# Gate rows made by TensorE transposes and stored as whole rows, and the weights' check as one tensor_reduce

## The chip, the cores and the metric

The kernel runs on one core of a Trainium2 chip. The time is device microseconds of one launch, from host buffers already in the device's memory to the finished output. The kernel before takes 1070.4 us, the median of 3 runs (1067.88 to 1073.14).

## The reference

Three layers follow each other. The first is attention over 4 batches, 8 heads, 768 positions and 64 channels, with a window of 96 local keys, 8 global keys and a distance bias. The second is a dense layer on 3072 tokens, where `cos` stands for the activation. The third is a mixture of 8 experts with a skip gate. The gate rows of the change are the 8 columns of `w_gate` and the vector `w_skip`, nine vectors of 512 numbers in all.

```python
scores = scale * np.matmul(q, k.transpose(0, 1, 3, 2))      # masked, biased, softmax over keys
x = attention(q, k, v)                                      # 3072 x 512
h = x @ w_in;  g = h * np.cos(h);  x = g @ w_out            # d_ff = 2048
skip_score = x @ w_skip
logits = x[skip_score > 0] @ w_gate                         # 8 experts, argmax picks one
out = x;  out[do] += gate_w * (relu(x @ w1[e]) @ w2[e])
```

The weights `w_in` and `w_out` reach the kernel as 64-bit floats and are turned into 32-bit floats on the chip. The check of the change belongs to that: it notes, for every piece of weights, how small its smallest absolute value is, so that a slower path can be taken for values too small for the fast conversion.

## The kernel before

Tokens are worked on in 8 units (u = 0 to 7) of 384 tokens. Attention takes a unit's heads in 4 pairs (p = 0 to 3). For a pair, `att_Tq` and `att_Tk` turn Q and K over on TensorE, `att_S` multiplies them (6 products, each reduced by VectorE on L380), `att_E` takes exponentials on ScalarE and scales on GpSimd (L404), `att_P` turns the result over, and `att_V` multiplies it with V. I write S(2) for the products of unit 0's pair 2, and likewise V(3), and so on; pair p of unit 1 is (1,p).

Unit 0's attention runs first, as a prologue. Then `unit(0)` does 16 steps f of the dense layer: 12 matmuls into `hp` (L499), the activation, 9 matmuls into `zp` (L538). In the steps of one unit the next unit's attention is interleaved. While unit 0 runs, the weights are converted, in 32 pieces of 128x512 numbers. A piece is loaded into a tile `st` (L202, 4 buffers). `convert` then runs ScalarE on L210, and VectorE on L216 (the check), L223 and L227; `convert_end` adds on GpSimd (L234). Step f waits for its pieces, so unit 0 is the unit in which conversion and the dense layer go side by side. From unit 1 on the weights lie in SBUF.

The gate rows are loaded as columns into `wgs` (L736 and L737) and written to a DRAM tile `wg_t` (L739), whence one broadcast load brings them as rows to all partitions after unit 0 (`wrep`, L833).

All loads of the prologue stand in one queue, issued by SyncE in order; one issue waits for the DMA that stands eight before it, and for its buffer. A scheduler sets the order on SyncE, VectorE and GpSimd, also in the prologue on ScalarE and TensorE; TensorE's order from unit 0 on, and ScalarE's in the units, is as written.

Of the kernel before, what the change touches and what calls it, by code (L numbers as in the profile page):

```python
# [9 lines left out]
F32 = mybir.dt.float32  # L10
F32R = mybir.dt.float32r
BF16 = mybir.dt.bfloat16
# [3 lines left out]
ALU = mybir.AluOpType  # L16
AX = mybir.AxisListType
# [3 lines left out]
P = 128  # L21
# [16 lines left out]
def kernel(  # L38
    ctx, tc, q, k, v, n_global, n_local, w_in, w_out, w_skip, w_gate, w1, w2, out
):  # L40
    nc = tc.nc
    B, H, S, D = q.shape
    NT, DM = out.shape
    FF = w_in.shape[1]
    E, _, F2 = w1.shape
    NP = H // 2
    CC = DM // P
# [9 lines left out]
    NG = 16  # L57
# [5 lines left out]
    drp = ctx.enter_context(tc.tile_pool(name="drp", bufs=1, space=DRAM))  # L63
    ps_h = ctx.enter_context(tc.tile_pool(name="ps_h", bufs=2, space=PSUM))
    ps_z = ctx.enter_context(tc.tile_pool(name="ps_z", bufs=HT, space=PSUM))
    ps_a = ctx.enter_context(tc.tile_pool(name="ps_a", bufs=3, space=PSUM))
# [10 lines left out]
    ident = cpool.tile([P, P], F32, name="ident")  # L77
# [7 lines left out]
        out=upper, in_=ones, pattern=[[1, P]], base=0, channel_multiplier=-1,  # L85
        compare_op=ALU.is_gt, fill=0.0,
    )
    wgs = cpool.tile([P, CC, NG], F32, name="wgs")
# [12 lines left out]
    for j, a in enumerate((n_global, n_local)):  # L101
# [11 lines left out]
        out=lim, in0=lim_h, scalar=2.0 ** 32, in1=lim, op0=ALU.mult, op1=ALU.add  # L113
# [19 lines left out]
        out=loc, in0=rel, scalar=nlo, in1=dst, op0=ALU.is_lt, op1=ALU.mult  # L133
# [14 lines left out]
    def to_far(d, kept):  # L148
# [12 lines left out]
        out=dst_f, in0=tmp, scalar=nlo, in1=dst[:, 104:NW], op0=ALU.mult, op1=ALU.add  # L161
# [6 lines left out]
        out=dst[:, 0:8], in0=g8[:, 0:8], scalar1=nlo, scalar2=None, op0=ALU.mult  # L168
# [9 lines left out]

    xs = drp.tile([E * CAP, ROW], F32, name="xs")

    wg_t = drp.tile([E + 1, DM], F32, name="wg_t")

    def rows_of(e):
        return xs[e * CAP:e * CAP + NE, :].rearrange("(j p) r -> p j r", p=P)
# [13 lines left out]
    cmin = cpool.tile([P, 2 * FC], F32, name="cmin")  # L198
# [6 lines left out]
    def convert(st, dst, pool, n=None):  # L205
        def shaped(t):
            return t.rearrange("p (a b) -> p a b", b=P)

        b = pool.tile([P, 512], I32, name="cvb", bufs=2)
        nc.scalar.activation(out=b, in_=st[:, :, 0].bitcast(U32), func=AF.Copy, scale=2.0 ** -29)  # L210
        u = pool.tile([P, 512], BF16, name="cvu", bufs=2)
        hf = st[:, :, 1].bitcast(F32)
        if n is None:
            nc.scalar.activation(out=u, in_=hf, func=AF.Abs)
        else:
            nc.vector.tensor_tensor_reduce(  # L216
                out=u, in0=hf, in1=hf, op0=ALU.mult, op1=ALU.max, scale=-1.0, scalar=-3.0e38,
                accum_out=cmin[:, n:n + 1],
            )
        if dst is None:  # L220
            dst = shaped(st[:, :, 0]).bitcast(F32)
        hi, a = shaped(st[:, :, 1]), dst.bitcast(I32)
        nc.vector.tensor_scalar(  # L223
            out=a, in0=hi, scalar1=3, scalar2=0x3FFFFFF8,
            op0=ALU.logical_shift_left, op1=ALU.bitwise_and,
        )
        nc.vector.scalar_tensor_tensor(  # L227
            out=a, in0=hi, scalar=-0x40000000, in1=a, op0=ALU.bitwise_and, op1=ALU.bitwise_or
        )
        return dst, shaped(b), None if n is not None else shaped(u)  # L230
# [16 lines left out]
    def spare_tile():  # L247
        x = cp_.tile([P, 512, 2], I32, name="st", bufs=4).bitcast(F32)
        return x.rearrange("p n two -> p (n two)")
# [11 lines left out]
    def conv_tick():  # L261
        if len(conv_run) == 3 or (conv_run and conv_run[0][3] == 2):
            m, f, parts, _ = conv_run.pop(0)
            conv_done.add((m, f))
            if m == 1:
                hi, lo = (w[:, f].rearrange("p (a b) -> p a b", b=P) for w in (wo_hi, wo_lo))
                nc.scalar.copy(hi, parts[0])  # L267
                nc.vector.tensor_tensor(out=lo, in0=parts[0], in1=hi.bitcast(F32), op=ALU.subtract)  # L268
        for c in conv_run:
            if c[3] == 1:  # L270
                c[3] = 2
                convert_end(*c[2])
        conv_ahead(2)
        if conv_loaded:
            m, f, st = conv_loaded.pop(0)
            dst = work_place(f) if m else w_in_sb[:, :, f * P:(f + 1) * P]
            conv_run.append([m, f, convert(st, dst, cp_, 2 * f + m), 1])
        conv_ahead(1)
# [456 lines left out]
    att_load(0, 1)  # L735
    nc.sync.dma_start(wgs[:, :, 0:E], w_gate.rearrange("(c p) e -> p c e", p=P))  # L736
    nc.sync.dma_start(wgs[:, :, E:E + 1], w_skip.rearrange("(c p o) -> p c o", p=P, o=1))  # L737
    for e in range(E + 1):
        nc.sync.dma_start(wg_t[e].rearrange("(c p) -> p c", p=P), wgs[:, :, e])  # L739
    warm(16, ps_a, "ps")  # L740
    att_Tq(0, 0)
    att_Tk(0, 0)
    for p in range(NP + 1):
        if p + 1 < NP:
            att_Tq(0, p + 1)
            att_Tk(0, p + 1)
        if p < NP:
            for t in range(HT):
                att_S(0, p, t)
            if p + 1 < NP:  # L750
                fill(p + 1)
            if p + 2 < NP:
                att_load(0, p + 2)
            att_E(0, p)
        warm(2, ps_a, "ps")
        if p > 0:
            for t in range(HT):
                att_P(0, p - 1, t)
                if t > 0:
                    att_V(0, p - 1, t - 1)  # L760
            att_V(0, p - 1, HT - 1)
        conv_tick()

    def early():
        for s_ in range(min(list(ev) + list(late)), 0):
# [43 lines left out]
    is_low = cpool.tile([P, 2 * FC], BF16, name="is_low")  # L809
# [3 lines left out]
    def route_setup():  # L813
        nc.gpsimd.iota(slots, pattern=[[1, NE]], base=0, channel_multiplier=0,
                       allow_small_or_imprecise_dtypes=True)
        nc.gpsimd.iota(last_id, pattern=[[0, 1]], base=NT - P, channel_multiplier=1,
                       allow_small_or_imprecise_dtypes=True)
        side.close()
        rp_["p"] = route_pool.enter_context(tc.tile_pool(name="route", bufs=2, side="right"))

        nc.vector.tensor_scalar(
            out=is_low, in0=cmin, scalar1=-(1.125 * 2.0 ** -15) ** 2, scalar2=None, op0=ALU.is_gt
        )

        def count_low():
            lp = ps_a.tile([P, 2 * FC], F32, name="ps_w2", tag="ps")
            nc.tensor.matmul(lp, ones, is_low, start=True, stop=True)
            nc.vector.tensor_reduce(out=low, in_=lp, op=ALU.max, axis=AX.X)

        at(HS + 10, count_low)  # L830
        gp_ = rp_["g"] = gate_pool.enter_context(tc.tile_pool(name="gate", bufs=1, side="right"))
        wrep = gp_.tile([P, E + 1, DM], F32, name="wrep", bufs=1)
        nc.sync.dma_start(  # L833
            wrep.rearrange("p e d -> p (e d)"),
            wg_t.rearrange("(o e) d -> o (e d)", o=1).to_broadcast([P, (E + 1) * DM]),
        )
        Route.wrep = [wrep[:, e] for e in range(E + 1)]

# [91 lines left out]
    with tc.manual_schedule(engines={mybir.EngineType.PE}):  # L930
# [8 lines left out]
        with tc.manual_schedule(engines={mybir.EngineType.SP}):  # L939
            with tc.manual_schedule(engines={mybir.EngineType.Activation}):  # L940


                u = NU - 1
# [69 lines left out]
                with tc.manual_schedule(engines={mybir.EngineType.Pool, mybir.EngineType.DVE}):  # L1013
                    with tc.manual_schedule(engines={mybir.EngineType.Activation}):
# [17 lines left out]
                        def trans_x0(cs):  # L1032
# [16 lines left out]
                            out=sel, in0=slots, scalar1=r.sf[:, 0], scalar2=None, op0=ALU.is_equal  # L1049
# [15 lines left out]
                    for n in range(NS + LAG):  # L1065
                        e, f = divmod(n, F2C)
# [13 lines left out]
                        if n >= LAG:  # L1080
                            e, f = divmod(n - LAG, F2C)
# [35 lines left out]
        out=ctl[:, 1:2], in0=ctl[:, 4:5], scalar1=float(NE), scalar2=None, op0=ALU.is_gt  # L1117
# [276 lines left out]
```

## Time and profile before

| what | value |
|---|---|
| median of 3 runs | 1070.4 us |
| the profiled execution's own time | 1068.65 us |
| its span, first to last instruction | 1066.9 us |
| mean granted TensorE clock | 0.964 of full speed |
| busy TensorE / VectorE / GpSimd / ScalarE | 977.0 / 751.2 / 543.2 / 529.0 us |

The chain of work that ended last is 56% TensorE and 27% VectorE over the whole span, but that is an average over stages. The prologue lasts to 72.6 us, unit 0 to about 201.6 us. A busy figure counts an instruction from its start to its end, so one that stands still within counts as busy.

### The profile page before, as it was taken

How to read it: one execution, taken by the hardware profiler on the slowest of the kernel's cores; microseconds unless marked ns; L12 is line 12 of the kernel's file. 1: busy time of each engine (PE TensorE's matmuls, PEld its weight loads, DVE VectorE, ACT ScalarE, POOL GpSimd, SP SyncE). 2: the span in 40 equal slices, each digit the busy share in tenths (PEclk: the TensorE clock that was granted, in tenths of full speed). 3: DMA queues.
4: the chain of work that ended last, by engine and by line, in shares of the span. 5: the costliest groups of instructions: out<-in, count | busy, mean ns of one | idle time of the engine just before them, and what ended most of it. 6: DMA issues, size and time to landing. Idle time of an engine off the chain costs nothing.

```text
span 1066.9 us, 17010 instructions
## 1 busy us (share of the span) xinstructions
PE 977.0 (92%) x5673; PEld 806.2 (76%) x5673; DVE 751.2 (70%) x1867; ACT 529.0 (50%) x1278; POOL 543.2 (51%) x727
## 2 busy tenths in 40 slices
PE   6487787999998999999899999989998989999996
PEld 3265666777787788788677878877798879999995
DVE  5369899878569648855965795597456178888883
ACT  4366466655665666556556756656556111111110
POOL 2356877745444454544444445535546065556562
PEclk9578889999999999999999999999999999999998
DMA  6465445641121112112111211110003169555600
GB/s 65 98 193 151 126 131 144 182 149 27 39 70 25 36 47 68 27 40 66 29 29 48 63 30 39 39 45 14 11 30 145 53 232 353 191 195 194 214 23 23
DMA packets 135792, 98.28 MB, mean 92 GB/s; under 512 B 103959, under 2 KB 112151, under 8 KB 135568
## 3 DMA queue, kind: packets, MB, share of 16 engines
q1 hardware_dynamic: 132496, 91.13, 29.1%
q0 software_dynamic: 3200, 5.98, 1.5%
q8 instruction: 47, 0.77, 0.3%
q14 instruction: 49, 0.40, 0.1%
HBM read 80.58 MB, written 21.03 MB: 95 GB/s over the span
## 4 chain that ended last, share of the span: by engine, by line
PE 56%; DVE 27%; POOL 7%; issue 3%; DMA 2%; ACT 2%; SPq 1%; POOLq 0%; ACTq 0%; DVEq 0%
PE hp L499 14%; PE zp L538 14%; DVE junk L596 9%; PE hp L905 8%; PE zp L924 8%; DVE wi_lo L465 4%; POOL sc L404 3%; PE ps_s L375 3%; DVE cvu L216 2%; DVE r L482 2%; DVE sc L380 2%; DVE w_in_sb L223 2%; DVE r L525 2%; DVE w_in_sb L227 2%; POOL wi_hi L462 1%
## 5 line engine op out<-in xcount | busy, mean ns | idle before, releaser
L510 POOL TENSOR_TENSOR glo<-r,ghi 128x384 fp32r<-128x384 f32 x115 | 128.9, 1121 | 201.2 <-ACT ghi L509 200.9
L465 DVE TENSOR_TENSOR wi_lo<-w_in_sb,wi_hi 128x512 fp32r<-128x512 f32 x124 | 104.8, 845 | 117.1 <-POOL wi_hi L462 112.4
L499 PE MATMUL hp<-xhi,wi_hi 128*128 128x384 f32 x492 | 177.4, 361 | 9.0 <-DVE r L525 6.0
L499 PE MATMUL hp<-xhi,wi_lo 128*128 128x384 f32 x492 | 167.0, 339 | 2.7 <-DVE wi_lo L465 2.7
L499 PE MATMUL hp<-xlo,wi_hi 128*128 128x384 f32 x492 | 166.4, 338 | 0.0
L538 PE MATMUL zp<-wo_hi,ghi 128*128 128x512 f32 x345 | 148.9, 432 | 0.4 <-ACT wo_hi L267 0.4
L487 ACT ACTIVATE r<-r,halfpi 128x384 f32<-128x384 f32 x128 | 79.0, 617 | 134.8 <-DVE r L482 133.4
L596 DVE CUSTOM_DVE_ANT_0 junk<-r_zr,wrep 128x512 bf16<-128x512 f32 x162 | 139.1, 858 | 7.4 <-ACT r_zr L558 5.3
L538 PE MATMUL zp<-wo_hi,glo 128*128 128x512 f32 x345 | 138.7, 402 | 2.6 <-POOL glo L510 2.6
L538 PE MATMUL zp<-wo_lo,ghi 128*128 128x512 f32 x345 | 138.7, 402 | 1.4 <-DVE wo_lo L268 1.4
L404 POOL TENSOR_SCALAR sc<-sc,sm 128x232 f32<-128x232 f32 (+1 forms) x180 | 93.5, 538 | 75.5 <-DVE sm L399 60.1
L509 ACT CAST ghi<-r 128x384 fp32r<-128x384 f32 x115 | 58.9, 512 | 110.8 <-DVE r L525 110.1
L499 PEld LDWEIGHTS hp<-xhi,wi_hi 128*128 128x128 f32 x492 | 93.1, 189 | 25.6 <-issue 13.1
L462 POOL TENSOR_SCALAR wi_hi<-w_in_sb 128x512 fp32r<-128x512 f32 x128 | 92.0, 719 | 39.3 <-PE hp L499 34.0
L375 PE MATMUL ps_s<-kW,qT 64*128 64x232 f32 (+1 forms) x384 | 76.2, 416 | 25.0 <-DVE mx L380 11.2
L910 ACT ACTIVATE hh<-hp 128x256 fp32r<-128x256 f32 x64 | 24.5, 383 | 149.9 <-PE hp L905 149.9
L499 PEld LDWEIGHTS hp<-xhi,wi_lo 128*128 128x128 f32 x492 | 93.1, 189 | 3.4 <-DVE wi_lo L465 3.4
L499 PEld LDWEIGHTS hp<-xlo,wi_hi 128*128 128x128 f32 x492 | 93.4, 190 | 0.1
L394 ACT ACTIVATE sc<-sc,mx 128x232 f32<-128x232 f32 (+1 forms) x180 | 83.3, 464 | 4.3 <-DVE mx L380 3.9
L525 DVE TENSOR_TENSOR r<-r,hp 128x384 f32<-128x384 f32 x112 | 61.6, 550 | 33.5 <-ACT r L487 33.5
L843 POOL TENSOR_SCALAR w2h<-we 128x512 fp32r<-128x512 f32 x64 | 47.2, 738 | 69.4 <-PE zp L924 69.4
L538 PEld LDWEIGHTS zp<-wo_hi,ghi 128*128 128x128 f32 x345 | 66.7, 193 | 19.7 <-issue 8.6
(232 smaller groups left out, 2252.1 us busy)
## 6 DMA issues: line engine op xcount, KB each, us to landing
we<-in_moe_w_dram SPq DMA_DIRECT2D x16, 2048.0 KB
st<-in_moe_w_in_dram SPq DMA_DIRECT2D x16, 512.0 KB
st<-in_moe_w_out_dram SPq DMA_DIRECT2D x16, 512.0 KB
ld_q<-in_q_dram SPq DMA_DIRECT2D x64, 96.0 KB
ld_k<-in_k_dram SPq DMA_DIRECT2D x64, 96.0 KB
ld_v<-in_v_dram SPq DMA_DIRECT2D x64, 96.0 KB
out_dram<-r_zr SPq DMA_DIRECT2D x7, 768.0 KB
xs<-st SPq DMA_DIRECT2D x16, 257.0 KB
```

The costliest lines, as they stand in the source:

```text
L375: nc.tensor.matmul(sp[:, c0:NW], d["qT"][j * D:(j + 1) * D, t * P:(t + 1) * P], d["kW"][j * D:(j + 1) * D, t, c0:NW], start=True, stop=True,)
L394: nc.scalar.activation(out=s[:, j, c0:NW], in_=s[:, j, c0:NW], func=AF.Exp, scale=-1.0, bias=d["m"][:, t, j:j + 1], accum_out=sm[:, t, j:j ...
L404: nc.gpsimd.tensor_scalar(out=s[:, j, c0:NW], in0=s[:, j, c0:NW], scalar1=sm[:, t, j:j + 1], scalar2=1.0, op0=ALU.mult, op1=ALU.mult,)
L462: nc.gpsimd.tensor_scalar(out=hi, in0=ws, scalar1=1.0, scalar2=1.0, op0=ALU.mult, op1=ALU.mult)
L465: eng.tensor_tensor(out=lo, in0=ws, in1=hi.bitcast(F32), op=ALU.subtract)
L499: nc.tensor.matmul(hp, a[:, c, :], b[:, c, :], start=(n == 0), stop=(n == 3 * CC - 1))
L510: nc.gpsimd.tensor_tensor(out=glo, in0=r, in1=ghi.bitcast(F32), op=ALU.subtract)
L525: nc.vector.tensor_tensor(out=r, in0=r, in1=hp, op=ALU.mult)
L538: nc.tensor.matmul(zt[u][t], a[:, sl], b[:, f, :], start=(f == 0 and n == 0), stop=(f == FC - 1 and n == 2),)
L596: nc.vector.tensor_tensor_reduce(out=junk, in0=self.zr[:, t, 0:DM], in1=self.wrep[e], op0=ALU.mult, op1=ALU.add, scale=1.0, scalar=0.0, ac ...
L905: nc.tensor.matmul(hp, a[:, c, :], b[:, c, :], start=(n == 0), stop=(n == 3 * CC - 1))
L924: nc.tensor.matmul(yq[e][j], a[:, sl], b, start=(f == 0 and n == 0), stop=(f == F2C - 1 and n == 2),)
```

## The change

The check becomes a `tensor_reduce` with minimum over absolute values, which gives the least absolute value instead of the negated least square; the compare on L821 is adapted, and the scratch tile `cvu` is no longer allocated for it. The nine stores of gate columns (L739) go. In their place, after the prologue's loop, four transposes on TensorE turn the 16 columns of `wgs` into 16 rows of 512 in PSUM, ScalarE copies them into a borrowed `st` tile, and one DMA stores them to `wg_t`, which now has 16 rows.

```diff
         b = pool.tile([P, 512], I32, name="cvb", bufs=2)
         nc.scalar.activation(out=b, in_=st[:, :, 0].bitcast(U32), func=AF.Copy, scale=2.0 ** -29)
-        u = pool.tile([P, 512], BF16, name="cvu", bufs=2)
         hf = st[:, :, 1].bitcast(F32)
         if n is None:
+            u = pool.tile([P, 512], BF16, name="cvu", bufs=2)
             nc.scalar.activation(out=u, in_=hf, func=AF.Abs)
         else:
-            nc.vector.tensor_tensor_reduce(
-                out=u, in0=hf, in1=hf, op0=ALU.mult, op1=ALU.max, scale=-1.0, scalar=-3.0e38,
-                accum_out=cmin[:, n:n + 1],
+            nc.vector.tensor_reduce(
+                out=cmin[:, n:n + 1], in_=hf, op=ALU.min, axis=AX.X, apply_absolute_value=True
             )
...
-    for e in range(E + 1):
-        nc.sync.dma_start(wg_t[e].rearrange("(c p) -> p c", p=P), wgs[:, :, e])
     warm(16, ps_a, "ps")
...
+    gT = ps_a.tile([P, 512], F32, name="ps_g0", tag="ps")
+    for c in range(CC):
+        nc.tensor.transpose(gT[0:NG, c * P:(c + 1) * P], wgs[:, c, :], ident)
+    gr = spare_tile()[0:NG, 0:DM]
+    nc.scalar.copy(gr, gT[0:NG])
+    nc.sync.dma_start(wg_t, gr)
```

The scheduler orders the prologue anew around this. Below, lines of the changed kernel are mostly one lower than before (L302 is L301, L380 is L379). The first place is SyncE's queue behind the loads of `wgs`. Before, from the Q load of pair 2 on:

```order
L302 DMA ld_q<-in_q_dram 128x3x64 x2
L302 DMA ld_k<-in_k_dram 128x3x64
L739 DMA wg_t<-wgs 128x4x1 x9
L302 DMA ld_k<-in_k_dram 128x3x64
L310 DMA ld_va<-in_v_dram 8x2x64
L302 DMA ld_v<-in_v_dram 128x3x64 x2
```

The same place in the changed kernel:

```order
L301 DMA ld_q<-in_q_dram 128x3x64 x2
L301 DMA ld_k<-in_k_dram 128x3x64 x2
L202 DMA st<-in_moe_w_in_dram 128x4x256 x2
L301 DMA ld_q<-in_q_dram 128x3x64 x2
L301 DMA ld_k<-in_k_dram 128x3x64 x2
L202 DMA st<-in_moe_w_in_dram 128x4x256
```

The nine stores are gone from between the two halves of pair 2's K load, two pieces of weights follow at once, and Q and K of pair 3 come before V of pair 2.

The second place is GpSimd between the scaling of pair 1 (`xhi`) and that of pair 3 (`xlo`). Before:

```order
L404 TENSOR_SCALAR sc<-sc,sm 128x128 x2
L404 TENSOR_SCALAR sc<-sc,sm 128x232 x2
L234 TENSOR_TENSOR w_in_sb<-w_in_sb,cvb 128x4x128
L404 TENSOR_SCALAR sc<-sc,sm 128x232 x2
L462 TENSOR_SCALAR wi_hi<-w_in_sb 128x512
L234 TENSOR_TENSOR w_in_sb<-w_in_sb,cvb 128x4x128
L462 TENSOR_SCALAR wi_hi<-w_in_sb 128x512
L355 COPY kW<-keep 128x104
L356 COPY kW<-keep 128x2x8 x2
```

In the changed kernel:

```order
L233 TENSOR_TENSOR w_in_sb<-w_in_sb,cvb 128x4x128
L461 TENSOR_SCALAR wi_hi<-w_in_sb 128x512
L233 TENSOR_TENSOR w_in_sb<-w_in_sb,cvb 128x4x128
L461 TENSOR_SCALAR wi_hi<-w_in_sb 128x512
L355 COPY kW<-keep 128x2x8
L354 COPY kW<-keep 128x104
L355 COPY kW<-keep 128x2x8
L403 TENSOR_SCALAR sc<-sc,sm 128x128 x2
L403 TENSOR_SCALAR sc<-sc,sm 128x232 x4
```

The two conversion pieces and the small copies into `kW`, which S(3) needs, now stand ahead of the scaling of pair 2 (`sc`) and no longer behind it.

The third place is SyncE again, at the loads of unit 1's first pairs, in the changed kernel:

```order
L301 DMA ld_v<-in_v_dram 128x3x64 x2
L309 DMA ld_va<-in_v_dram 8x3x64
L766 DMA wg_t<-st 16x512
L314 DMA ld_va<-in_v_dram 96x3x64
L309 DMA ld_va<-in_v_dram 8x3x64
L314 DMA ld_va<-in_v_dram 96x3x64
L301 DMA ld_q<-in_q_dram 128x3x64 x2
```

The new store of the gate rows stands in the middle of pair (1,0)'s loads; pair (1,1), Q and K of pair (1,2) and the seventh piece of weights come behind it.

## Rows read from the trace of the kernel before

**Rows 1.** Waits, 14 to 72.6 us: who waited for whom; us, times, longest.
```profile
PE zp L341 <- DMA ld_k<-in_k_dram: 16.6, 1, 16.6
...
PE ps_s L375 <- POOL kW L356: 4.5, 1, 4.5
```

**Rows 2.** Chain that ended last, 14 to 75 us: start, us, what.
```profile
14.35 14.19 DMA wg_t<-wgs
28.55 9.11 DMA ld_k<-in_k_dram
...
37.79 0.89 PE zp L341 x3
...
54.42 2.78 PE ps_s L375 x8
...
67.98 0.47 DVE xlo L448
...
72.55 2.56 PE hp L499 x8
```

**Rows 3.** Stretches: range, length, busy per engine, granted clock, DMA share, GB/s.
```profile
14.00:38.00 24.00, 6.87 (x49) 4.21 (x49) 5.79 (x31) 6.28 (x25) 5.11 (x12) 0.70 0.53 22
38.00:72.60 34.60, 25.85 (x148) 17.11 (x147) 23.50 (x72) 19.83 (x63) 18.22 (x25) 0.70 0.59 158
72.60:201.60 129.00, 106.94 (x530) 82.20 (x530) 118.75 (x224) 77.93 (x179) 97.21 (x92) 0.87 0.49 142
201.60:1067.00 865.40, 827.21 (x4909) 697.85 (x4907) 595.58 (x1497) 419.64 (x1001) 420.24 (x583) 0.99 0.26 84
```

**Rows 4.** Timeline 0 to 30 us: start, us, engine, line, operation.
```profile
7.47 1.02 SPq L302 DMA_DIRECT2D ld_k<-in_k_dram  x2
...
10.78 0.55 PE L341 MATMUL zp<-ident,ld_k 128*128 128x128 f32 x3
```

**Rows 5.** Timeline of SyncE's issues, 10 to 240 us.
```profile
13.33 0.43 SPq L302 DMA_DIRECT2D ld_k<-in_k_dram  x1
13.86 10.37 SPq L739 DMA_DIRECT2D wg_t<-wgs  x9
...
65.50 1.00 SPq L302 DMA_DIRECT2D ld_q<-in_q_dram  x2
...
71.59 0.94 SPq L302 DMA_DIRECT2D ld_q<-in_q_dram  x2
...
73.71 0.42 SPq L202 DMA_DIRECT2D st<-in_moe_w_in_dram  x1
```

**Rows 6.** VectorE's groups by shape, 80 to 200 us: busy, mean ns, idle before.
```profile
L216 DVE CUSTOM_DVE_ANT_0 cvu<-st 128x512 bf16<-128x512 f32 x26 | 30.1, 1159 | 0.0
```

**Rows 7.** Durations by source line, whole run: ns min/median/max, first and last start.
```profile
L216 DVE CUSTOM_DVE_ANT_0 cvu<-st x32: 676/996/1789, 44.0 to 193.7; 128x512 bf16<-128x512 f32 x32
...
L223 DVE TENSOR_SCALAR w_in_sb<-st x28: 415/542/1503, 44.6 to 179.7; 128x512 int32<-128x512 int32 x28
...
L482 DVE SCALAR_TENSOR_TENSOR r<-r,hp x123: 490/547/556, 76.4 to 822.5; 128x384 f32<-128x384 int32 x123
```

**Rows 8.** Timeline of VectorE, 118 to 150 us.
```profile
125.78 1.50 DVE L216 CUSTOM_DVE_ANT_0 cvu<-st 128x512 bf16<-128x512 f32 x1
```

**Rows 9.** Timeline of GpSimd, 118 to 150 us.
```profile
125.27 1.47 POOL L510 TENSOR_TENSOR glo<-r,ghi 128x384 fp32r<-128x384 f32 x1
```

**Rows 10.** VectorE's groups by shape, whole run: reductions, and the check's second record.
```profile
L216 DVE DVE_READ_ACCUMULATOR2_ANT cmin<- 128x1 f32 x32 | 2.5, 78 | 0.0
...
L657 DVE TENSOR_REDUCE r_ss<-r_sl 128x3 f32<-128x24 f32 x7 | 1.2, 178 | 0.2
...
L645 DVE TENSOR_REDUCE r_gs<-r_ex 128x1 f32<-128x8 f32 x3 | 0.5, 157 | 0.0
```

**Rows 11.** ScalarE's groups by shape, whole run.
```profile
L558 ACT COPY r_zr<-zp 128x512 f32<-128x512 f32 x24 | 12.6, 589 | 21.8 <-PE zp L538 21.8
```

More of the change, by code (lines that the diff above doesn't have):

```diff
@@ L179 @@
     xs = drp.tile([E * CAP, ROW], F32, name="xs")
-    wg_t = drp.tile([E + 1, DM], F32, name="wg_t")
+    wg_t = drp.tile([NG, DM], F32, name="wg_t")
     def rows_of(e):
@@ L821, in route_setup @@
         nc.vector.tensor_scalar(
-            out=is_low, in0=cmin, scalar1=-(1.125 * 2.0 ** -15) ** 2, scalar2=None, op0=ALU.is_gt
+            out=is_low, in0=cmin, scalar1=1.125 * 2.0 ** -15, scalar2=None, op0=ALU.is_lt
         )
@@ L834, in route_setup @@
             wrep.rearrange("p e d -> p (e d)"),
-            wg_t.rearrange("(o e) d -> o (e d)", o=1).to_broadcast([P, (E + 1) * DM]),
+            wg_t[0:E + 1].rearrange("(o e) d -> o (e d)", o=1).to_broadcast([P, (E + 1) * DM]),
         )
```

## The prediction

> **What bounds the kernel now.** I read the stretches first, because the change touches only the first fifth of the run [rows 3]. Up to 201.6 us TensorE is far from full: 25.85 us busy of 34.60 in the second half of the prologue, 106.94 of 129.00 in unit 0, at a granted clock of 0.70 and 0.87. After it, TensorE is busy for 827.21 of 865.40 us at 0.99, and nothing there is timed from the launch. So what is saved before 201.6 us moves the end by as much, and what the change costs is also paid there.
>
> Then I read the waits of the prologue [rows 1]. The longest in the prologue is TensorE's for the K load of pair 2, 16.6 us, once. The reader is to see in the chain what it hides [rows 2]: 14.19 us go to `wg_t<-wgs`, 9.11 us to the K load behind it, and the turning of K goes on only at 37.79 us. The row of that stretch shows the engines of the DMA busy for 0.53 of the time while they move 22 GB/s, against 158 GB/s at a share of 0.59 afterwards [rows 3]. Nine stores of single numbers keep the queue full and move almost nothing.
>
> In unit 0 VectorE is the fullest, 118.75 of 129.00 us [rows 3]. The check is a large part of that: 26 of the 32 fall between 80 and 200 us, at a mean of 1159 ns [rows 6], though the shortest of all takes 676 ns [rows 7]. The timelines show why: the check that starts at 125.78 us and takes 1.50 us [rows 8] starts while GpSimd's L510 runs, from 125.27 for 1.47 us, to 126.74 [rows 9]; what is left after that, 125.78 + 1.50 - 126.74 = 0.54 us, is a little under the 676 ns. The check stood still until GpSimd was done.
>
> **Part 1: the hole in the prologue.** The K load of pair 2 is issued in two halves, at 13.33 us and, as the chain has it, at 28.55 us behind the nine stores [rows 2, 5]. In the changed order the halves stand together, so the second goes out at about 13.85 us. How fast it lands I take from pair 1: its K halves are issued from 7.47 us to 8.49, and K is turned from 10.78 on, at most 2.3 us after [rows 4]. Issued by 14.4 us, pair 2's K is then there by 16.7 us. By then TensorE stands at the first transposes of pair 0's result, and K is turned at about 17.4 us (an estimate: the landing, and an instruction or two ahead in its order) instead of 37.79. That is 20.4 us, if all else only shifts.
>
> More than a shift is likely. Before, S(3) starts at 54.42 us, 16.6 us after K of pair 2, and 4.5 us of that are a wait for GpSimd's small copy into `kW` [rows 1, 2]. That copy stood behind the scaling of pair 2, which needs S(2) and its exponentials; now it stands ahead of it, and Q and K of pair 3 are asked for earlier. Against it, 1 MB of weights is now queued ahead of these loads, and VectorE has two pieces to convert ahead of the reductions of S(2). I take 2.5 us, about half of that wait, between 0 and the whole 4.5 with the 1.5 us that the chain could give besides: 6. Part 1 is 20.4 + 2.5 = 23 us. The low end is 16: the shift less some 4 us, if the loads that the stores held back now meet. They are 24 us at 22 GB/s and 34.6 us at 158, together 6.0 MB up to the first dense matmul; at 158 GB/s all the time, 6.0 MB last 38 us, from 14 to 52 us. The forecast has the first dense matmul at 72.55 - 23 = 49.6 us, so this pace is near.
>
> **Part 2: the check.** No row shows a `tensor_reduce` of 512 numbers. From below, 415 ns, the shortest 128x512 operation with one source [rows 7]. From above, if the whole 178 ns of the reduction over 24 numbers were a price per number, 7.4 ns each, 512 would take 3.8 us [rows 10]. Between 8 and 24 numbers the reductions go from 157 to 178 ns, 1.3 ns a number with two more results written; that gives 157 + 504 x 1.3 = 820 ns, and with a share of the rise put down to the results less. I take 0.68 us, the shortest check of before [rows 7], because it too walks 512 numbers with the same stride and keeps one result.
>
> The other question is whether it stands still as the old check did. L223 has one source, in SBUF, and does: 415 to 1503 ns. But it is faster than 512 numbers at the pace of the old check. L482 has one source in SBUF and one in PSUM, and in 123 instances it stays between 490 and 556 ns [rows 7]. The reduce, with one source and no wide result, is nearer to L482. So each of the 26 goes from 1159 to 680 ns, 26 x 0.48 = 12.5 us on the engine that bounds this stretch. I count all of it, since VectorE is 92% busy there. At worst it stands still like the old one and only the second record goes, 26 x 78 ns = 2.0 us [rows 10]; at best GpSimd gains too, and the whole 26 x 676 ns = 17.6 us come back. The six checks of the prologue I count as nothing: VectorE is busy 23.50 of 34.60 us there [rows 3], and the reordered loads cover them; without that cover they would be worth as much each as the others, 6 x 0.48 = 2.9 us more.
>
> The Trainium skill, SBUF — State Buffer, section Who interferes with whom, has a rule for this: a VectorE instruction with two SBUF inputs, or in a two-port mode, is blocked while GpSimd holds the shared ports, and `tensor_reduce` on trn2 never is. The rows on L216, L223 and L482 agree with the first half; no run here shows the second. By that rule Part 2 is 12.5 us or more; if the rule were wrong, 2.0. Against the change speaks the Trainium skill, VectorE: DVE Perf Modes, section Rules for kernel authors: expect 1x of `tensor_reduce`, the slowest operation of this engine. By its rate, one number a cycle at 0.96 GHz, 512 numbers are 533 ns and a fixed part; an estimate of 0.69 us with the same page's 151 cycles, and the sum would be 12.2 us instead of 12.5.
>
> **Part 3: what is added.** Four transposes stand between the products of V(3), where TensorE waits for ScalarE's copies anyway; I put them at nothing, and without that cover a set of three of before takes 0.55 us [rows 4]. ScalarE's copy is like L558, 0.59 us [rows 11], ahead of unit 1's first Q, on the path: 0.6 us. The store moves 16 rows in place of 4608 single numbers: nothing.
>
> But its issue waits for that copy, in the middle of SyncE's queue, and pair (1,0)'s last loads, pair (1,1), Q and K of (1,2), and the seventh piece of weights stand behind it. Before, these went out while V(3) was still running: the loads of (1,1) from 65.50 us, Q and K of (1,2) from 71.59, the seventh piece at 73.71 [rows 5], 5.7 us after V(3)'s `xlo` at 67.98 [rows 2]. Now the store can go out about 0.6 us after the same point, and behind it come 1.2 us for three loads, 6.1 us (65.50 to 71.59) and 2.1 us (71.59 to 73.71): the piece goes out 10 us after. It is 4.3 us later against V(3). I take 2 us, between 0 (the conversion had slack) and 4.5. The borrowed `st` tile is one of four for as long as the store takes; that is in the same term.
>
> **Sum.** -23 - 12.5 + 0.6 + 2 = -32.9 us, from the profiled execution's 1068.65 us: 1035.8. That execution lay 1.75 us under the median of the runs; I add about half of that for the median: 1037 us. The likeliest case by itself: 1026 to 1046.
>
> **Rivals.**
> - *The wait moves on.* The reduce runs free, but GpSimd and VectorE take turns, and L223 or L227, next in order, stands still where the check did; only the second record is saved. For it: L223 already reaches 1503 ns. Against: GpSimd works on while the reduce runs. Then -23 - 2 + 2.6: 1046, with the median's part 1047. Chance 0.25.
> - *The jam is not the nine stores'.* The loads of the gate weights into `wgs` are just as finely cut and stay; if they fill the queue, the change doesn't close the hole. Then -12.5 + 2.6: 1059 or 1060. Against it: the chain names `wg_t`. Chance 0.04.
> - *Slower.* A reduce priced per number, on the check's place in unit 0: 26 + 6 of them on a full VectorE. Part 1 and the added terms leave 20.4 us to lose, so from 1.1 + 20.4 / 32 = 1.75 us each it decides. At the upper bound of 3.8 us it would be 32 x 2.7 = 86 us more, 66 us slower, 1135. Against it, the step from 8 to 24 numbers costs 21 ns, not 119. Chance 0.02.
> - *More.* Part 1 at 26, Part 2 at 17.6, no delay of the pieces: 1025 or 1026. Chance 0.14.
>
> The forecast has 0.55. Its bounds and those of the first and the last rival give the range: from 1024, with all best terms, to 1053, where the wait moves on and the loads set the pace (-16 - 2 + 2.6). A measurement of this kernel tells about 0.5%, 5 us, from no change. Every case but the slower one and a little of the second lies beyond that: faster 0.95, same 0.03, slower 0.02.
>
> **What the profile of the changed kernel would show.** Part 1 is right if TensorE turns K of pair 2 before 20 us, the first dense matmul stands at 45 to 53 us, and no wait over 5 us is left on a DMA in the prologue. Part 2 is right if L216 has a mean of 0.6 to 0.75 us with a largest value close to it, the means of L223 and L227 don't rise, and unit 0 (129.00 us now) takes about 118. If L216 ranges to 1.7 us, or L223 takes up what it gave, the first rival is true. Part 3 shows as the time from V(3)'s `xlo` to the seventh piece's issue, 10 us. The stretch after unit 0 should stay 865 us long; if it doesn't, something moved that I haven't seen.

## The result, and the profile after

The changed kernel takes 1040.8 us (median of 4 runs, 1037.8 to 1042.4) against 1071.8 us for the kernel before in the same series (4 runs, 1067.9 to 1073.9): a ratio of 0.9712, with a 95% interval of 0.9674 to 0.9750. A later series gave 1039.0 us (5 runs, 1035.3 to 1043.4), a ratio of 0.9706 (0.9682 to 0.9729). The forecast was 1037 us, so 3.8 and 2.0 us too low, well within its range.

Of the lines of the changed kernel, L226 is the L227 of the prediction, L222 its L223, L464 its L465; the check keeps L216. The first profiled run (1041.5 us, span 1039.6) reads as follows. First its page: the span, the busy time of the engines, and the DMA packets of the kernel's transfers (the last line is that of the kernel before, with 4720 packets more).

```profile
span 1039.6 us, 16982 instructions
...
PE 976.4 (94%) x5677; PEld 805.6 (77%) x5677; DVE 739.2 (71%) x1835; ACT 529.0 (51%) x1279; POOL 533.1 (51%) x727
...
q1 hardware_dynamic: 127776, 91.14, 29.2%
...
q1 hardware_dynamic: 132496, 91.13, 29.1%
```

Then the stretches that answer to [rows 3]: the prologue, unit 0, and what follows (columns as there).

```profile
14.00:51.66 37.66, 33.24 (x201) 20.97 (x200) 25.80 (x97) 25.43 (x86) 21.44 (x37) 0.82 0.56 143
51.66:173.30 121.64, 103.88 (x530) 80.94 (x530) 110.97 (x201) 79.33 (x181) 88.81 (x92) 0.89 0.54 156
173.30:1039.60 866.30, 829.42 (x4909) 698.89 (x4908) 595.28 (x1495) 418.88 (x1001) 420.43 (x583) 0.99 0.26 84
```

Unit 0 is taken here from its first dense product to the end of its last `wo_lo`. The row of [rows 3] ends one `wo_lo` sooner; between the same marks unit 0 of before reads:

```profile
72.48:202.30 129.82, 107.76 (x535) 82.62 (x534) 119.55 (x227) 78.75 (x179) 97.21 (x92) 0.87 0.49 142
```

So the first dense product comes 72.48 - 51.66 = 20.8 us sooner, unit 0 is 129.8 - 121.5 = 8.3 us shorter (its last `wo_lo` ends at 173.2), and the rest 1.8 longer: 27.3 us, the difference of the spans (1066.9 and 1039.6). The reader is to see two more things. TensorE is now busy for 33.24 of 37.66 us in the prologue, so the hole is gone. And in unit 0 VectorE's busy time fell by 119.55 - 110.97 = 8.6 us, while that of GpSimd, whose program was not changed, fell by 97.21 - 88.81 = 8.4.

The chain of the prologue (start, length, what) has no DMA until after the first dense product; K of pair 2 is turned at 20.15 us in it (37.79 in [rows 2]), the first dense product starts at about 51.7 (72.5).

```profile
15.11 3.14 PE ps_s L374 x12
...
20.15 0.65 PE zp L340 x3
...
50.44 1.29 PE ps_s L374 x6
51.73 3.84 PE hp L498 x12
56.94 4.48 DMA st<-in_moe_w_in_dram
61.44 0.69 DVE cmin L216
```

The check by its source line, over the whole run (ns min/median/max):

```profile
L216 DVE TENSOR_REDUCE cmin<-st x32: 645/674/686, 21.0 to 165.4; 128x1 f32<-128x512 f32 x32
```

VectorE's groups by shape in unit 0 (count, busy us, mean ns, idle before):

```profile
L226 DVE SCALAR_TENSOR_TENSOR w_in_sb<-st,w_in_sb 128x512 int32<-128x512 int32 x22 | 20.0, 908 | 0.1
L216 DVE TENSOR_REDUCE cmin<-st 128x1 f32<-128x512 f32 x26 | 17.5, 674 | 1.2 <-DMA st<-in_moe_w_in_dram 1.2
L222 DVE TENSOR_SCALAR w_in_sb<-st 128x512 int32<-128x512 int32 x22 | 17.1, 786 | 0.0
L267 DVE TENSOR_TENSOR wo_lo<-w_in_sb,wo_hi 128x512 fp32r<-128x512 f32 x12 | 12.3, 1027 | 0.3 <-ACT wo_hi L266 0.3
...
L222 DVE TENSOR_SCALAR st<-st 128x512 int32<-128x512 int32 x4 | 4.6, 1171 | 0.0
```

And two of GpSimd's groups there, with the second one's line of the kernel before at the end:

```profile
L233 POOL TENSOR_TENSOR w_in_sb<-w_in_sb,cvb 128x512 int32<-128x512 int32 x23 | 32.5, 1413 | 20.1 <-DVE w_in_sb L226 7.5 <-PE ps_s L374 4.2 <-ACT sc L393 3.3
...
L403 POOL TENSOR_SCALAR sc<-sc,sm 128x232 f32<-128x232 f32 x24 | 13.3, 570 | 11.5 <-DVE sm L398 11.5
...
L404 POOL TENSOR_SCALAR sc<-sc,sm 128x232 f32<-128x232 f32 x24 | 17.6, 750 | 7.1 <-DVE sm L399 7.1
```

A check takes 645 to 686 ns wherever it stands, where the old one took 676 to 1789 [rows 7]. In unit 0 the two groups of GpSimd had means of 1497 and 750 ns before, L227 900, L223 792 and, into `st`, 733, and L268 947. Counted from the two traces, the hold-up of the old check went both ways: of its 26 in unit 0 the 20 that started while GpSimd worked took 1302 ns on average, the other six 679; and of GpSimd's 24 scalings (L404) the five that started within a check took 1148 ns, the other 19 took 645. With the reduce, seven scalings started within a check and took 489 ns.

### The profile page after: what moved, and what is told of

It reads as the page before. It is cut to its first block, busy times and chain, and to the rows that moved or that the text cites. A ratio compares the mean times of both kernels' runs of the same rounds, so it can differ in the third digit from the quotient of the medians.

```text
span 1039.6 us, 16982 instructions
## 1 busy us (share of the span) xinstructions
PE 976.4 (94%) x5677; PEld 805.6 (77%) x5677; DVE 739.2 (71%) x1835; ACT 529.0 (51%) x1279; POOL 533.1 (51%) x727
## 4 chain that ended last, share of the span: by engine, by line
PE 58%; DVE 27%; POOL 6%; issue 3%; ACT 3%; DMA 1%; SPq 1%; POOLq 0%; ACTq 0%; DVEq 0%
PE hp L498 15%; PE zp L537 15%; DVE junk L595 9%; PE hp L909 9%; PE zp L928 9%; DVE wi_lo L464 4%; PE ps_s L374 3%; POOL sc L403 3%; DVE r L481 2%; DVE sc L379 2%; DVE r L524 2%; DVE w_in_sb L226 1%; POOL wi_hi L461 1%; DVE w_in_sb L222 1%; PE ps_p L415 1%
## 5 line engine op out<-in xcount | busy, mean ns | idle before, releaser
L509 POOL TENSOR_TENSOR glo<-r,ghi 128x384 fp32r<-128x384 f32 x115 | 128.5, 1118 | 202.8 <-ACT ghi L508 199.0
L464 DVE TENSOR_TENSOR wi_lo<-w_in_sb,wi_hi 128x512 fp32r<-128x512 f32 x124 | 104.0, 839 | 115.0 <-POOL wi_hi L461 108.7
L403 POOL TENSOR_SCALAR sc<-sc,sm 128x232 f32<-128x232 f32 (+1 forms) x180 | 88.1, 509 | 78.7 <-DVE sm L398 68.6
L374 PE MATMUL ps_s<-kW,qT 64*128 64x232 f32 (+1 forms) x384 | 75.7, 410 | 16.6 <-DVE mx L379 8.0
L847 POOL TENSOR_SCALAR w2h<-we 128x512 fp32r<-128x512 f32 x64 | 47.3, 738 | 69.3 <-PE zp L928 69.3
L537 PEld LDWEIGHTS zp<-wo_hi,ghi 128*128 128x128 f32 x345 | 66.4, 193 | 18.9 <-issue 8.3
```

Source lines behind the costliest of these rows:

```text
L374: nc.tensor.matmul(sp[:, c0:NW], d["qT"][j * D:(j + 1) * D, t * P:(t + 1) * P], d["kW"][j * D:(j + 1) * D, t, c0:NW], start=True, stop=True,)
L403: nc.gpsimd.tensor_scalar(out=s[:, j, c0:NW], in0=s[:, j, c0:NW], scalar1=sm[:, t, j:j + 1], scalar2=1.0, op0=ALU.mult, op1=ALU.mult,)
L464: eng.tensor_tensor(out=lo, in0=ws, in1=hi.bitcast(F32), op=ALU.subtract)
L509: nc.gpsimd.tensor_tensor(out=glo, in0=r, in1=ghi.bitcast(F32), op=ALU.subtract)
L537: nc.tensor.matmul(zt[u][t], a[:, sl], b[:, f, :], start=(f == 0 and n == 0), stop=(f == FC - 1 and n == 2),)
```

## The experiments

**Each part alone.** The first kernel has the gate rows of the change and the old check:

```diff
-            nc.vector.tensor_reduce(
-                out=cmin[:, n:n + 1], in_=hf, op=ALU.min, axis=AX.X, apply_absolute_value=True
-            )
+            nc.vector.tensor_tensor_reduce(
+                out=u, in0=hf, in1=hf, op0=ALU.mult, op1=ALU.max, scale=-1.0, scalar=-3.0e38,
+                accum_out=cmin[:, n:n + 1],
+            )
```

> Gate rows as in the changed kernel, the weights' check as before. Theory (the two parts are separate, and the hole belongs to the nine column stores alone): the first dense product starts at 51.7 us as in the changed kernel (before 72.5), unit 0 keeps its 129 us plus about 2 for the store that SyncE waits with, so 1071.8 - 20.8 + 2 = about 1053 us. Rival (the parts help each other, since a faster check is what lets the shorter prologue be used): unit 0 longer than 133 us and the time over 1057 us. Rival (the check is worth its whole sum of 12.5 us and the gate rows the rest): 1041 + 12.5 = 1053 as well, told apart only with the run of the check alone.

Measured: 1053.6 us, ratio 0.9821 (0.9781 to 0.9860), first dense product at 52.6 us, unit 0 130.6 us. The second kernel has the new check and the nine column stores of before:

```diff
-    nc.sync.dma_start(wg_t, gr)
+    for e in range(E + 1):
+        nc.sync.dma_start(wg_t[e].rearrange("(c p) -> p c", p=P), wgs[:, :, e])
```

> The least absolute value by a reduce, the nine column stores as before. Theory: the hole stays (first dense product at 72.5 us), VectorE's busy time in unit 0 falls by less than the 14.6 us that the check loses, since its other instructions grow longer; unit 0 goes from 129 to about 119.5 us without the store's block, so 1071.8 - 9.5 = about 1062 us. Rival (the sum of the prediction: nothing is given back): unit 0 at 117 us, 1059 us. Rival (another engine takes the wait over, so that the gate rows gave everything): 1069 to 1072 us.

Measured: 1060.2 us, ratio 0.9865 (0.9823 to 0.9907), first dense product at 74.7 us. The unit 0 rows of both, the gate rows alone first:

```profile
52.63:183.20 130.57, 105.67 (x530) 80.96 (x530) 119.74 (x227) 79.33 (x181) 97.82 (x92) 0.89 0.51 148
```

```profile
74.69:195.70 121.01, 101.16 (x535) 78.77 (x534) 111.60 (x201) 79.61 (x181) 89.62 (x92) 0.94 0.53 152
```

The savings of 1.79% and 1.35% add up to 3.14%, against 2.88% (2.50 to 3.26) for both together: the parts are separate, as far as these intervals tell. Each stretch belongs to one part: the hole goes with the stores, and unit 0's 9 us and GpSimd's 8 us go with the check. By the medians the check alone is worth 13.6 us, by unit 0's length in the traces 8.8 to 9.6 (129.8 or 130.6 against 121.0); the interval of the ratio, 10 to 19 us, doesn't quite reach that, and this is left open. The profiled run of the check alone was the slowest of its four (1062.5 against 1057.2 to 1061.7 us), and what the six checks of the prologue are worth no pair of these traces shows: the granted clock in the prologue differs between them (see the repeat of the changed kernel below).

**Form and place of the stores.** The nine column stores, but at the new, later place in SyncE's queue:

```diff
-    gT = ps_a.tile([P, 512], F32, name="ps_g0", tag="ps")
...
-    nc.sync.dma_start(wg_t, gr)
+    for e in range(E + 1):
+        nc.sync.dma_start(wg_t[e].rearrange("(c p) -> p c", p=P), wgs[:, :, e])
```

> The changed kernel, but the gate rows are stored as nine columns again, at the later place (behind the last loads of unit 0, in front of those of unit 1's pair (1,0)). Theory (the jam comes from the number of packets, wherever the stores stand): the first dense product stays near 50 to 52 us, since the loads of unit 0 are ahead of the stores; the loads and the 7th piece of the weights behind them land 14 us later or more (the 7th piece after 65 us instead of 61), and unit 0 ends 4 to 14 us later: 1045 to 1055 us. Rival (only the place mattered): within 2 us of the changed kernel, 1039 to 1043 us.

Measured: 1066.6 us, ratio 0.9923 (0.9896 to 0.9950); unit 0 121 us long, as with the new check elsewhere, but the first dense product at 72.8 us. Its chain:

```profile
36.89 10.81 DMA wg_t<-wgs
48.13 18.89 DMA ld_q<-in_q_dram
67.15 0.87 PE ps_t L330 x3
...
72.91 3.69 PE hp L498 x12
```

Now it is Q of unit 1's pair (1,0) that lands 18.9 us after its issue. So the jam belongs to the form, not to the place, and it hits whatever load comes behind. The theory was right on that and wrong on where it would show: TensorE has the transposes and S of pair (1,0) ahead of the first dense product in its order, so that waited too, and the loss was some 23 us (ratio 0.9923 against 0.9712; 26 by the medians), not 4 to 14.

The converse, whole rows at the early place (the block of transposes, copy and store moved up as it is):

```diff
     warm(16, ps_a, "ps")
     att_Tq(0, 0)
     att_Tk(0, 0)
+    gT = ps_a.tile([P, 512], F32, name="ps_g0", tag="ps")
...
+    nc.sync.dma_start(wg_t, gr)
```

> The changed kernel with the four transposes, the copy and the whole-row store put where the column stores stood, in front of the loads of pair 2. Theory (the packets' number made the jam, and the place only makes waits): no wait of the kind ld_k of 16 us comes back, but TensorE and SyncE now wait for wgs to land and for the copy, so ld_q and ld_k of pair 2 go out about 5 us later (19 us) and the first dense product starts 2 to 4 us later (54 to 56 us); unit 0 loses its 2 us of block; 1041 to 1043 us. Rival (any store of the gate rows at this place jams the loads, whatever its form): the first dense product near 70 us, 1058 us or more.

Measured: 1037.2 us, ratio 0.9659 (0.9622 to 0.9696); first dense product at 54.2 us, unit 0 117.3 us. The jam does not come back, and SyncE was not even held: its timeline shows the loads of pair 2 and a piece of weights ahead of the store.

```profile
13.34 0.96 SPq L301 DMA_DIRECT2D ld_k<-in_k_dram  x2
...
15.94 0.34 SPq L745 DMA_DIRECT2D wg_t<-st  x1
```

But TensorE was held: its timeline shows 3.2 us of waiting for `wgs`.

```profile
14.24 1.01 PE L742 MATMUL ps_g<-ident,wgs 128*16 128x128 f32 x4 [3.22 <-DMA wgs<-in_moe_w_skip_dram]
```

The stretch behind that wait has a granted clock of 0.50 (the number in front of the DMA share). That is no mark of this kernel: the first run of the changed kernel, without that wait, has 0.50 from 10.8 to 21.0 us.

```profile
15.00:22.00 7.00, 6.92 (x28) 4.60 (x26) 4.10 (x18) 5.33 (x17) 0.78 (x1) 0.50 0.96 257
```

**SyncE's block.** The changed kernel, with the store issued by ScalarE:

```diff
-    nc.sync.dma_start(wg_t, gr)
+    nc.scalar.dma_start(wg_t, gr)
```

> The changed kernel with the gate rows' store issued from ScalarE, which makes the copy, so that SyncE is not held from 40.2 to 48.1 us. Theory (the block delays the 7th piece of the weights and with it unit 0's conversion): the 7th piece goes out at about 50 us instead of 56.9, the first check of unit 0 starts by 56 us instead of 61, unit 0 is 2 us shorter (0 to 4): about 1039 us. Rival (the piece waits for its staging buffer, or VectorE has other work there): issue at 55 us or later, 1040.8 us, no change.

Measured: 1039.1 us, ratio 0.9682 (0.9642 to 0.9722). The 7th piece goes out at 52.9 us, 2.9 us after the first dense product (at 50.0) instead of 5.3; the first check of unit 0 starts at 58.9, 9.0 us after it instead of 9.8. Unit 0 is as long as before the edit, 121.3 us. But the edit did not free SyncE, it moved the block: in the changed kernel SyncE waits 7.8 us for ScalarE's copy, here 3.7 us, until 48.2 us, for the landing of the very store, with the issue of a V load (SyncE's waits from 40 to 60 us: who waited for whom; us, times, longest):

```profile
SPq L301 <- DMA wg_t<-st: 3.7, 1, 3.7
```

So the run doesn't show what the block costs; it shows that a shorter and later one gives no gain that a measurement can tell.

**What the check costs now.** The changed kernel without the check (its result set to a constant once), and with the check of unit 0's 26 pieces done twice:

```diff
-            nc.vector.tensor_reduce(
-                out=cmin[:, n:n + 1], in_=hf, op=ALU.min, axis=AX.X, apply_absolute_value=True
-            )
+            pass
```

> The changed kernel without the weights' check: the check's instruction is left out and its result set to a constant once. Theory (VectorE's work per piece still sets the pace of unit 0's conversion; the old check against the new one moved the stretch from the first piece of unit 0 to the last by 9.6 us for 14.6 us of VectorE's time, 0.66 for one): 17.5 us less of VectorE's time is 11.5 us less: about 1029 us. Rival (GpSimd or TensorE has become the bound): 3 us less at most, 1038 us or more.

```diff
+            for _ in range(1 if n in (0, 1, 2, 3, 4, 6) else 2):
                 nc.vector.tensor_reduce(
```

> The changed kernel with the check of each of the 26 pieces of unit 0 done twice (same result): 17.5 us more of VectorE's time. Theory (0.66 for one): 11.5 us more, 1052 us. Rival (VectorE sets the pace alone, one for one): 17.5 us more, 1058 us. Rival (the time is elsewhere): 1041 to 1044 us.

Measured: without the check 1043.4 us, ratio 0.9708 (0.9680 to 0.9736), no gain that shows; twice 1046.8 us, ratio 0.9734 (0.9706 to 0.9761), which is 2 to 3 us above the changed kernel's ratio where 11.5 us were expected. My 0.66 for one fell on both sides. Without the check, the stretch of unit 0, and then three groups of VectorE in it:

```profile
52.60:176.00 123.40, 103.19 (x544) 81.54 (x543) 101.03 (x177) 79.07 (x181) 88.50 (x92) 0.92 0.55 156
```

```profile
L221 DVE TENSOR_SCALAR w_in_sb<-st 128x512 int32<-128x512 int32 x22 | 19.9, 910 | 1.5 <-DMA st<-in_moe_w_in_dram 1.1 <-DMA st<-in_moe_w_out_dram 0.2
L266 DVE TENSOR_TENSOR wo_lo<-w_in_sb,wo_hi 128x512 fp32r<-128x512 f32 x12 | 13.4, 1118 | 1.0 <-ACT wo_hi L265 1.0
...
L463 DVE TENSOR_TENSOR wi_lo<-w_in_sb,wi_hi 128x512 fp32r<-128x512 f32 x12 | 14.7, 1229 | 12.2 <-POOL wi_hi L460 10.1 <-PE hp L497 2.1
```

With the check twice, the same two views:

```profile
51.97:179.50 127.53, 103.01 (x535) 80.22 (x534) 121.01 (x227) 80.07 (x181) 89.23 (x92) 0.89 0.53 152
```

```profile
L217 DVE TENSOR_REDUCE cmin<-st 128x1 f32<-128x512 f32 x52 | 34.9, 673 | 1.0 <-DMA st<-in_moe_w_in_dram 1.0
...
L223 DVE TENSOR_SCALAR w_in_sb<-st 128x512 int32<-128x512 int32 x22 | 16.0, 729 | 0.0
L268 DVE TENSOR_TENSOR wo_lo<-w_in_sb,wo_hi 128x512 fp32r<-128x512 f32 x12 | 9.9, 828 | 0.0
```

The same two operations take 910 and 1118 ns with no reduce per piece, 786 and 1027 with one, 729 and 828 with two; not every operation follows (L226 of the changed kernel: 930, 908 and 959). All records of VectorE in unit 0 but the check's add up to 110.5, 107.1 and 102.2 us: what is taken from the check is partly given to the others, and the other way round. (Another 2.5 to 4 us of the 17.5 were never to be had, since successive records overlap by some 0.07 us each.) So VectorE's busy time falls by 9.9 us without the reduces and rises by 10.0 with twice as many. GpSimd's busy time is the same in all three (88.5, 88.8, 89.2 us), against 97.2 and 97.8 with the old check. And the strongest pair: two reduces per piece take more of VectorE (34.9 us) than the old check with its second record (29.0 + 2.0 us beside the same gate rows), yet unit 0 is 3.0 us shorter with them, 127.5 against 130.6; the medians are 1046.8 and 1053.6, the ratios 0.9734 and 0.9821. TensorE's clock is the same in both stretches (0.89), and VectorE's busy time nearly so (121.01 and 119.74 us).

**Room in the prologue.** Between 42 and 61 us VectorE takes up no new piece in the changed kernel. The store from ScalarE, and three more steps of the conversion in the prologue:

```diff
         conv_tick()
+        if p >= 2:
+            conv_tick()
```

> The store from ScalarE, and three more steps of the conversion in the prologue (one more after each of pairs 2, 3 and the last round), so that the 7th piece of the weights is asked for ahead of unit 1's loads. Theory (unit 0 ends some 111 us after its conversion takes up again, and VectorE has room for it between 41 and 59 us): pieces 7 to 9 are checked before 55 us, and unit 0 ends 5 to 10 us sooner; 1029 to 1034 us. Rival (VectorE's attention work in the prologue is as much on the chain, so the conversion pushes the first dense product back by what it gains): 1037 to 1041 us.

Measured: 1039.8 us, ratio 0.9672 (0.9642 to 0.9701). Pieces are checked from 44 to 51 us, as the theory had it, and unit 0 shrinks to 114 us; but the first dense product moves from 50.0 to 56.5, behind a 4.0 us wait of S for VectorE's reduction. The rival is right on the time, and VectorE is busy for 12.96 of the 15.47 us from 41 us on. How much of the 6.5 us is VectorE's is not separated: this run has a granted clock of 0.50 from 11.7 to 21.9 us and again from 35.6 to 42.4 and from 52.7, the one it is compared with only from 24.2 to 31.0.

**Side by side.** The same steps with the rows at the early place, the changed kernel, and the early place alone, in five rounds on one chip:

> Whole rows made and stored at the early place (1037.2 us in its own run), and the three more steps of the conversion in the prologue. Theory (the two savings add up: 1.6 us and 3.1 us at unit 0's end against the changed kernel, by their traces): unit 0 ends at about 168 us, 3 to 5 us under the changed kernel on the same chip. Rival (both use the same room of VectorE between 41 and 60 us, so the first dense product moves back by what is gained): within 1.5 us of the early place alone.

> The changed kernel itself, unaltered, to have it beside the variants on one chip. Expected 0.9712 of the kernel before, as first measured (0.967 to 0.975). If it comes out at 0.966 or less, the early place and the store from ScalarE are no gain.

> Whole rows at the early place, once more, beside the changed kernel on one chip. Theory (the late place holds SyncE for 8 us and delays the 7th piece): 2 to 4 us under the changed kernel. Rival (the first dense product 2.5 us later cancels it, and the 1037.2 us was the chip's): within 1.5 us of it.

Measured: 1039.9, 1039.0 and 1038.3 us; ratios 0.9701 (0.9683 to 0.9720), 0.9706 (0.9682 to 0.9729), 0.9681 (0.9656 to 0.9705). No variant is told apart from the changed kernel; the 1037.2 us of the early place was not repeated, and the second saving adds nothing.

The repeat of the changed kernel gave more than its time. Its profiled run has a span of 1033.4 us, 6.2 shorter than the first, of the same program, and 4.5 of that lie in the prologue. Three stretches of the first run, then of the second (the column in front of the DMA share is the granted clock):

```profile
12.00:15.00 3.00, 2.71 (x10) 0.95 (x6) 2.32 (x16) 2.58 (x12) 0.20 (x1) 0.50 0.62 106
15.00:18.30 3.30, 3.30 (x14) 2.26 (x14) 2.15 (x15) 2.27 (x10) 0.96 (x3) 0.50 0.87 231
...
40.00:47.00 7.00, 6.31 (x33) 3.57 (x33) 2.12 (x4) 1.66 (x5) 4.50 (x9) 0.61 0.23 43
```

```profile
12.00:15.00 3.00, 2.43 (x13) 1.33 (x14) 2.89 (x20) 2.79 (x13) 0.20 (x1) 1.00 0.61 104
15.00:18.30 3.30, 3.29 (x21) 2.25 (x21) 3.15 (x18) 3.10 (x13) 2.30 (x6) 1.00 0.88 245
...
40.00:47.00 7.00, 5.76 (x46) 3.80 (x46) 1.98 (x9) 4.28 (x14) 2.26 (x5) 1.00 0.13 31
```

In the first run TensorE's clock stood at 0.50 (1.2 GHz) from 10.8 to 21.0 us and again from 41.6 to 48.4; in the second it stood at 1.00 (2.4 GHz) throughout the prologue. What TensorE did before 12 us is in the timelines, the first run's first:

```profile
1.16 5.04 PE L287 MATMUL ps_w<-ones 128*128 128x512 bf16 x16 [1.16 <-DVE ones L83]
...
9.70 0.52 PE L330 MATMUL zp<-ident,ld_q 128*128 128x128 f32 x3 [2.65 <-DMA ld_q<-in_q_dram]
...
15.04 3.21 PE L374 MATMUL ps_s<-kW,qT 64*128 64x128 f32 x12
...
19.94 0.85 PE L340 MATMUL zp<-ident,ld_k 128*128 128x128 f32 x3
```

```profile
1.16 6.59 PE L287 MATMUL ps_w<-ones 128*128 128x512 bf16 x16 [1.16 <-DVE ones L83]
...
9.77 0.52 PE L330 MATMUL zp<-ident,ld_q 128*128 128x128 f32 x3 [1.38 <-DMA ld_q<-in_q_dram]
...
14.00 2.42 PE L374 MATMUL ps_s<-kW,qT 64*128 64x128 f32 x12
...
17.28 0.49 PE L340 MATMUL zp<-ident,ld_k 128*128 128x128 f32 x3
```

Its first 16 matmuls were over sooner in the first run, and it stood idle for 2.65 us before pair 1's Q came, instead of 1.38. With the full clock the first dense product starts at 47.2 us; unit 0 is 121.5 us long in both runs, at a clock of 0.89 and of 0.96, so TensorE's clock doesn't set its length. The same two cases run through the other traces: of the eleven in which no column stores stand ahead of K of pair 2, four turn it at 17.1 to 17.3 us, with a clock of 1.00 from 15 to 18.3 us, and seven at 19.8 to 20.4, with 0.50. So the first dense product of two traces can be compared only with the clock beside it: the 50.0 us with the store from ScalarE belong to the four, as do the 52.6 us of the gate rows alone and of the kernel without the check, all three with 0.50 for a while after 23 us, and the first run's 51.7 to the seven.

## Why the prediction was right, and where not

**Part 1, the hole: right, with an open part in the overlap.** No wait over 5 us is left on a DMA, and the form of the stores made the jam, as the run with late columns shows against the run with early rows. The forecast had K of pair 2 turned at 17.4 us, 20.4 us sooner, and 2.5 us from the overlap. The second profiled run has 17.28 us, 20.5 sooner, and the first dense product 72.5 - 47.2 = 25.3 us sooner, so 4.8 us beyond the shift (2.5 were taken, 6 was the bound). The first run has K 17.6 us sooner, at 20.15 us and so just past the "before 20 us" of the prediction, and the dense product 20.8: the missing 2.8 us of the shift are the low clock, not a load, since TensorE waits for no DMA between 10.3 us and K in either. So 23 lies between the two. The wait for `kW` that the forecast named is nearly gone (4.5 us before, 0.5 and 0.3 in the two runs), but the gain beyond the shift isn't overlap alone: in the kernel before, TensorE's clock stood at 0.50 from 23.4 us, while it waited, to 47.3, and from 50.8 to 61.0, and in the second run never. The prediction read 0.70 in the prologue of before and made no term of it; how the 3.2 and 4.8 us divide is open.

**Part 2, the check: the duration right, the price wrong.** 674 ns against 680 forecast, and it never stands still. The Trainium skill, SBUF — State Buffer, section Who interferes with whom, says that a reduce never contends with GpSimd on this chip: the 32 rows of 645 to 686 ns agree. But unit 0 came out at 121.5 us, not 118. The step that failed is "I count all of it, since VectorE is 92% busy there", and with it the sign that "the means of L223 and L227 don't rise": the four L223 into `st` went from 733 to 1171 ns, L268 from 947 to 1027, L227 from 900 to 908. Of 30.1 + 2.0 - 17.5 = 14.6 us that the check's records gave up, VectorE's busy time shows 8.6: its other records went from 103.0 to 107.1 us in sum, and 1.9 us had been overlap of records. The conversion in unit 0, from its first check to the start of its last `wo_lo`, went from 121.2 to 111.1 us (120.2 against 111.7 with either part alone), so the check is worth 8.5 to 10 us there, not 12.5.

What the check held of the path can be read from the chain that ended last, which gives each line's share of a stretch. Unit 0 of the kernel before (72.48 to 201.6 us), then of the changed kernel (51.66 to 172.5), the lines as the view cuts them off:

```profile
by line: DVE cvu L216 16.1%; DVE w_in_sb L227 11.6%; DVE w_in_sb L223 11.3%; DVE wo_lo L268 6.8%; DVE wi_lo L465 6.6%; POOL sc L404 6.1%; issue 5.1%; DVE r L482 4.3%; DVE r L525 4.0%; POOL w_in_sb L234 3.6%; DVE sc L380 3.5%; PE hp L499 2.6
...
by line: DVE w_in_sb L226 12.1%; DVE w_in_sb L222 11.3%; DVE cmin L216 8.6%; PE hp L498 7.7%; DVE wo_lo L267 7.5%; DVE wi_lo L464 6.8%; issue 4.9%; DVE r L481 4.2%; DMA st<-in_moe_w_in_dram 3.7%; DVE sc L379 3.7%; PE zp L537 3.6%; DVE r L52
```

The check held 20.8 us of the path (16.1% of 129.1) and holds 10.4 (8.6% of 120.8), in the second run too. So 10.4 us left the path, not 12.5, and since unit 0 is 8.3 us shorter, some 2 us came back elsewhere on it; the path now holds 4.5 us (4.0 in the second run) of loading the seventh piece, where that of the kernel before has no load.

VectorE's time alone doesn't price this. Without the check, 17.5 us less of it gave nothing: VectorE then stands idle for 22 us of unit 0, 10 of them in front of `wi_lo` for GpSimd's `wi_hi`, and no other engine is full; what bounds unit 0 then stays open. And the way from the old check to the reduce has two steps: from the old check to two reduces, where VectorE's busy time stays and GpSimd's falls by 8.6 us, unit 0 is 3.0 us shorter; from two reduces to one, where VectorE's falls by 10.0 and GpSimd's stays, another 5.9. By the ratios the first step is about 0.9% and the second 0.2 to 0.3%, each with an uncertainty near 0.4 or 0.5%. So both the end of the hold-up, of which GpSimd's relief is one side, and the shorter check have a part, and how the gain divides between them is not shown. GpSimd's share of the path doesn't settle it: it is 15.8 us before, 7.0 in the first run of the changed kernel and 16.0 in the second, whose unit 0 is as long.

**Part 3, what is added: right in place, small in price.** ScalarE's copy took 0.57 us (0.6 forecast). The 7th piece went out 56.94 - 47.65 = 9.3 us after V(3)'s `xlo`, in the second run too (10 forecast, 5.7 before). The conversion of unit 0 starts 9.8 us after the first dense product instead of 7.9: 1.9 us, against 2 taken. What of this is the block's is not shown, since the store from ScalarE only moved it. The second run shows that it can be on the path: there the chain runs from the copy (43.4 us) through the store and 17 more issues of SyncE to that of the seventh piece at 52.72 us, its landing and the first check at 56.72.

**The rest.** The stretch after unit 0 is 866.4 and 864.7 us long in the two runs, against 864.6. Of the rivals, "the wait moves on" was half true: the other instructions did take up 4.1 of the 14.6 us, but L223 and L227 right behind the check only a part of them; the conversion still got 8.5 to 10 us, not 2. "The jam is not the stores'" is refuted by the late columns, and "slower" by 674 ns.

The forecast sum, 32.9 us, was met by the second run's span (33.5 us less) by luck, by two errors that cancel: Part 1 gave 25.3 instead of 23, unit 0 and what follows 8.2 instead of 9.9. In the first run both fell short.

## What to carry to other kernels

Stores of single numbers cost whatever stands behind them in the queue, wherever they are put: look for a stretch with a busy DMA that moves almost nothing, and make the rows whole on TensorE. Price an edit by what the instruction holds of the path, read from the chain, and not by its shorter duration times the count: where two engines stretch each other's instructions, the neighbours take a part of it. Before two traces are compared, look at the granted clock of both, stretch by stretch, and at an edit that is meant to take a wait away, look whether the wait is gone. And check with a run that leaves the edited work out whether there is still something to be had on that engine; here there was not.

## What the runs showed of the hardware

- The same program's prologue ended at 51.7 or at 47.2 us, with TensorE at a granted clock of 0.50 from 10.8 to 21.0 and 41.6 to 48.4 us, or at 1.00 throughout. These 4.5 us are more than the medians of the variants of place and issue lie apart (1037.2 to 1040.8 us).
- Nine stores, 4608 single numbers in all, delay the load behind them at either place: TensorE waited 16.6 us for K in the kernel before (from the first store's issue at 13.9 us to K's landing 23.8 us), and 20.8 us for Q of (1,0) with the columns stored late (30.6 us from 36.4).
- A VectorE operation of 128x512 on SBUF that takes 384 ns at best (L222) had means of 910, 786 and 729 ns in unit 0 with zero, one and two reduces per piece beside it: more of VectorE's time in reduces, which no instruction of GpSimd was seen to stretch, goes with less hold-up of its neighbours.
